# Attention and feed-forward on one core: fewer, wider warming matmuls at the front, and k^T v one block sooner in three units

## The chip, the cores and the metric

The kernel runs on one core of one Trainium2 chip. Time is device microseconds of one execution, from the program's start to its end on that core; less is better. The engines are TensorE (PE in the profile; its weight loads are listed apart as PEld), VectorE (DVE), ScalarE (ACT), GpSimd (POOL) and SyncE (SP). Each runs its own list of instructions in order, and they wait for each other through semaphores. Operands lie in SBUF (128 partitions); TensorE writes to PSUM[...].

## The reference

Linear attention with a norm, followed by a feed-forward layer:

```python
batch, n_heads, seq, head_dim = (8, 8, 576, 64)          # q, k, v in fp32
kv = np.einsum('bhsd,bhse->bhde', k, v)                  # "k^T v", 64x64 per batch and head
out = np.einsum('bhsd,bhde->bhse', q, kv)
rms = np.sqrt(np.mean(out * out, axis=-1, keepdims=True) + 1e-06)
attn_out = (out / rms * g_norm)
x = attn_out.transpose(0, 2, 1, 3).reshape(4608, 512)
h = x @ w_in                                             # 512 x 2048
g = s * np.maximum(h, 0.0) ** 2 + b
return g @ w_out                                         # 2048 x 512
```

All matmuls are in fp32. The weights arrive in pairs of 32-bit words, from which ScalarE (lines 235 and 240) and VectorE (lines 245 and 255) make fp32 values.

## The kernel before, in words

**Units.** The 4608 rows of x are nine units of 512 rows (u = 0 to 8). A unit is its first product (x w_in), the activation, and its second product (g w_out). Both products are done with fewer block products than plain tiling needs, from sums and differences of blocks (`mm1`, `mm1_deep`, `mm2`), except that three quarters of unit 0's first product are plain (`mm1_plain`). The attention rows of unit u + 1 are worked out beside unit u, in two pairs of 256 rows named A and B (`attention_of_two`: `turn`, `product`, `back`, `square`, `row_sum`, `norm`, `turn_x`, `scale`).

**k^T v.** `kv_product(b)` makes the eight 64x64 products of one batch b. A pass over i = 0, 1 takes four heads each; in each, nine steps j over the sequence, two pairs l and two row halves r give 36 matmuls of 64x64, so that four of them sit in different quarters of TensorE's array at once. The result goes through two PSUM banks (`kv_ps`) into `bd_kv[b % 2]`, a block-diagonal matrix, by four copies (ScalarE, line 402; for b = 0 two are on VectorE, line 400). Batch 0 is done at the front; b = 1 in the second product of unit 0; b = 2 in the first product of unit 1; b = 3 at the end of the second product of unit 1; b = 4 to 7 in the first products of units 3 to 6.

**The order of the work** is written out by hand; each engine gets its instructions in the order of the calls. For units 2 and up, `run` in `mm1_deep` lists the calls of the first product, and `at(n)` marks the places where side work is put in; `sides` tells which side work goes where. Around the change it reads, with `x1`, `x6`: four matmuls of 256 columns each and a ScalarE copy; `small(...)`: one level deeper, two matmuls of 128 columns per step:

- `at(4)`: A's `product`, 32 matmuls into two PSUM banks of the pool `ps_t` (line 554)
- `at(5)`: A's `back`, two VectorE transposes out of these banks (line 566), `square` on ScalarE (line 573) and B's `turn` on VectorE (line 542)
- `small(7, 0, 1, 2)`, `small(2, 0, 6, 7)`, `x6(1)`, then `at("kv")`: `kv_product` in units 3, 4 and 6, into the same two banks of `ps_t`, and then `small(7, 0, 6, 7)`

Unit 5 has its k^T v at `at(2)`, and into other banks. k and v for it come through a ring of 14 SBUF slots (`queue_w2`, `pump`, `used`), which SyncE's queue fills in the order of a list: for each unit k and v first, then the weights of the unit. `used` after k^T v frees its slots and lets SyncE issue the next loads.

**The front.** k and v of batch 0 are loaded in two halves (i = 0, 1), each by four transfers shared by the queues of SyncE and ScalarE, then q for the first 512 rows (eight transfers), then the first five weight blocks of 1 MB (SyncE, line 205). Meanwhile `warm` issues matmuls of an identity matrix into a PSUM tile that nobody reads. Before the first half of k^T v there are 18 of 128 columns; between the halves there are four of 128 columns and 42 of 4 columns. After the second half come, for four groups of 128 rows c = 0 to 3: `turn` (transposes of q, line 436), `take` (a copy on VectorE, line 441, or ScalarE, line 443), `product` (lines 92 and 452), `square`, `root`, `norm` (ScalarE lines 463 and 469, VectorE lines 465, 473 and 475), `turn_x` (lines 493 to 509), mixed with the conversion of the first two weight blocks (`hi`, `lo` on ScalarE, `shift`, `plus` on VectorE), and then the first plain products.

The program's list for TensorE has 3,924 matmuls before the change, 24 of them transposes, and 407 separate semaphore waits. In the trace, one matmul of the code is two LDWEIGHTS and two MATMUL records, and a transpose is one of each.

## Time and profile before

| what | us |
|---|---|
| median of three runs | 901.99 (901.68 to 902.92) |
| the profiled execution: its own time | 901.62 |
| the profiled execution: span from first to last instruction | 899.8 |
| TensorE busy in the span | 890.1 (99%) |
| VectorE busy | 697.8 (78%) |
| ScalarE busy | 354.1 (39%) |
| GpSimd busy | 262.7 (29%) |
| mean granted TensorE clock | 0.998 |

A row of the timeline has the start and the length in us, the engine, the line of the kernel, the operation, the tile written and the tiles read, the shape, the number of records merged, and, in brackets, how long the engine had been idle and what ended it. "issue" there means that the engine waited for nothing that the profile shows. Matmuls overlap, so a row's length reaches a little into the next row; the distance of two starts is the time that a row takes. In a table by stretch, each engine has its busy time and number of records, and then come the granted clock, the DMA share and GB/s.

The kernel's chain of work lies on TensorE for 95% of the span; VectorE has 3% of it, and DMA, ScalarE and "issue" 1% each.

### The profile page before, as it was taken

To read this page: it belongs to the slowest core of one execution; us is meant where nothing else is said; L and a number is where in the kernel's file an instruction comes from. 1 tells how busy PE (TensorE), PEld (TensorE's weight loads), DVE (VectorE), ACT (ScalarE), POOL (GpSimd) and SP (SyncE) were. 2 spreads that over 40 slices of the span, in tenths; PEclk is the share of its full clock that TensorE was granted. 3 is DMA by queue.
4 is the path that set the end of the run, shared out by engine and by line. 5 is a ranking of instruction groups with operands and counts; after the bars stand their busy time and mean duration, and the time that the engine had idled before them with its cause. 6 is when DMAs were issued, how large, how long until landed. Compare 5 with 4: busy or idle time off the path is not lost.

```text
span 899.8 us, 20172 instructions
## 1 busy us (share of the span) xinstructions
PE 890.1 (99%) x7824; PEld 826.6 (92%) x7824; DVE 697.8 (78%) x1374; ACT 354.1 (39%) x612; POOL 262.7 (29%) x493
## 2 busy tenths in 40 slices
PE   8999999999999999999999999999999999999998
PEld 7788888888899998999899999999999989999998
DVE  1899778786597977797788878897779787975696
ACT  1887124531266105630455026701761066205610
POOL 2017147213664023800472037403530300021000
PEclk9999999999999999999999999999999999999999
DMA  9797828539973996389656984597639822993286
GB/s 263 256 341 237 238 70 281 179 105 338 300 229 84 303 327 177 91 257 309 204 136 192 305 280 108 136 323 243 192 99 308 299 78 59 295 306 102 60 280 189
DMA packets 124110, 192.98 MB, mean 214 GB/s; under 512 B 25712, under 2 KB 43504, under 8 KB 124016
## 3 DMA queue, kind: packets, MB, share of 16 engines
q1 hardware_dynamic: 104048, 165.84, 58.4%
q0 software_dynamic: 16512, 23.63, 9.3%
q10 hardware_dynamic: 3456, 2.23, 1.0%
q8 instruction: 62, 1.02, 0.5%
q14 instruction: 32, 0.26, 0.1%
HBM read 164.37 MB, written 27.26 MB: 213 GB/s over the span
## 4 chain that ended last, share of the span: by engine, by line
PE 95%; DVE 3%; DMA 1%; ACT 1%; issue 1%; DVEq 0%; ACTq 0%
PE x_ps L92 46%; PE y_ps L92 25%; PE z_ps L92 11%; PE sx_ps L92 6%; PE st_ps L92 2%; PE kv_ps L386 2%; PE y_ps L554 2%; DMA kv_sb<-in_v_dram 1%; PE warm_ps L92 0%; DVE xT L598 0%; DVE xn L587 0%; DVE xs L263 0%; DVE ss L465 0%; PE z_ps L386 0%; DVE xn L475 0%
## 5 line engine op out<-in xcount | busy, mean ns | idle before, releaser
L1694 POOL DMA_DIRECT2D q_sb<-in_q_dram x296 | 167.2, 573 | 85.7 <-ACT r L928 44.1
L1274 POOL DMA_DIRECT2D out_dram<-o x120 | 59.6, 503 | 354.7 <-issue 210.5
L92 PE MATMUL x_ps<-w_sb,sub 128*128 128x128 f32 x1176 | 148.5, 275 | 0.0
L92 PEld LDWEIGHTS x_ps<-w_sb,sub 128*128 128x128 f32 x1176 | 139.8, 192 | 0.0
L653 ACT ACTIVATE a<-a,b_col,s_col 128x512 f32<-128x512 f32 x144 | 117.0, 813 | 27.0 <-DVE a L656 18.6
L853 ACT COPY a<-x_ps 128x512 f32<-128x512 f32 x28 | 16.3, 582 | 243.1 <-PE x_ps L92 243.1
L92 PE MATMUL x_ps<-xs,ws_raw 128*128 128x256 f32 x384 | 91.1, 380 | 0.1
L92 PE MATMUL x_ps<-xT,wa 128*128 128x256 f32 x360 | 84.1, 382 | 0.1
L92 PE MATMUL y_ps<-xs,wb 128*128 128x256 f32 (+1 forms) x360 | 80.0, 365 | 0.0
L92 PEld LDWEIGHTS x_ps<-xs,ws_raw 128*128 128x128 f32 x384 | 69.5, 190 | 8.3 <-ACT r L727 0.5
L92 PEld LDWEIGHTS x_ps<-xT,wa 128*128 128x128 f32 x360 | 66.6, 190 | 10.7 <-issue 1.7
L966 ACT ACTIVATE a<-a 128x512 f32<-128x512 f32 x112 | 69.6, 621 | 5.5 <-DVE a L267 5.5
L92 PEld LDWEIGHTS y_ps<-xs,wb 128*128 128x128 f32 x360 | 62.9, 190 | 9.1 <-issue 2.3
L92 PE MATMUL x_ps<-w_sb,a 128*128 128x128 f32 (+1 forms) x432 | 64.9, 298 | 0.0
L92 PE MATMUL y_ps<-w_sb,a 128*128 128x128 f32 (+1 forms) x416 | 62.4, 295 | 0.0
L92 PEld LDWEIGHTS x_ps<-w_sb,a 128*128 128x128 f32 x432 | 58.4, 192 | 2.9 <-issue 0.4
L92 PEld LDWEIGHTS y_ps<-w_sb,a 128*128 128x128 f32 x416 | 56.0, 192 | 2.1
L260 DVE TENSOR_TENSOR r<-sx_ps,a 128x256 f32<-128x256 f32 x84 | 35.3, 420 | 22.4 <-PE sx_ps L92 22.0
L260 DVE TENSOR_TENSOR r<-x_ps,o 128x256 f32<-128x256 f32 (+1 forms) x84 | 29.7, 354 | 28.4 <-PE x_ps L92 27.7
L92 PE MATMUL y_ps<-w_sb,sub 128*128 128x128 f32 x392 | 49.5, 275 | 0.0
L92 PE MATMUL z_ps<-w_sb,a 128*128 128x128 f32 (+1 forms) x352 | 46.9, 280 | 0.0
L263 DVE TENSOR_TENSOR a<-a,a 128x512 f32<-128x512 f32 x72 | 46.7, 683 | 0.1
(232 smaller groups left out, 1659.0 us busy)
## 6 DMA issues: line engine op xcount, KB each, us to landing
w_sb<-w SPq DMA_DIRECT2D x427, 256.0 KB, 4.9
w_sb<-w SPq DMA_DIRECT2D x14, 512.0 KB, 9.9
w<-sub POOLq DMA_DIRECT2D x28, 256.0 KB, 6.0
out_dram<-o POOLq DMA_DIRECT2D x112, 64.0 KB, 4.4
w_sb<-in_k_dram SPq DMA_DIRECT2D x24, 288.0 KB, 5.2
w_sb<-in_v_dram SPq DMA_DIRECT2D x24, 288.0 KB, 5.3
w_raw<-in_moe_w_in_dram SPq DMA_DIRECT2D x6, 1024.0 KB, 6.8
q_sb<-in_q_dram POOLq DMA_DIRECT2D x160, 32.0 KB, 3.9
```

What stands on the lines that cost most here:

```text
L92: nc.tensor.matmul(o, lhsT=lhsT, rhs=rhs, start=start, stop=stop, skip_group_check=True)
L260: nc.vector.tensor_tensor(out=o, in0=a, in1=b, op=ALU.add)
L263: nc.vector.tensor_tensor(out=o, in0=a, in1=b, op=ALU.subtract)
L386: nc.tensor.matmul(ps[r][(r ^ l) * HB : (r ^ l) * HB + HB, i, :], lhsT=kv[l][0][rows, j, :], rhs=kv[l][1][rows, j, :], start=(j == 0), sto ...
L554: nc.tensor.matmul(ps[l][32 * p : 32 * p + 32, r, lo:hi], lhsT=bd_kv[b % 2][rows, p, at : at + 32], rhs=st["qT"][rows, p, lo:hi], start=Tr ...
L653: nc.scalar.activation(t, t, AF.Identity, scale=s_col, bias=b_col)
L853: nc.scalar.copy(g_tile("a11", s), st["x", s])
L966: nc.scalar.square(ga[name, s], ga[name, s])
L1274: queues[s % 2].dma_start(out=view[b, jj, :, cols], in_=st[name, j][s * w : s * w + w, cols])
L1694: load()
```

## The change

`warm` makes matmuls of 512 columns: the identity matrix is read four times side by side as the moving operand, by a broadcast, and a whole PSUM bank is written. Before the first half of batch 0's k^T v there are four of them, for 18 of 128 columns; between the halves one, for four of 128 and 42 of 4. So TensorE's list has 59 matmuls less. In `run`, the place `at("kv")` goes ahead of `x6(1)`; it holds side work in units 3, 4 and 6 only. The lists of the other engines have the same instructions; on ScalarE the four copies of k^T v in these units change places with the copy of `x6(1)`. All lines after 362 move up by one or two.

```diff
-    def warm(n, tiny=0):
+    def warm(n):
 
         ps = ps_f.tile([P, 2, TB], FP32, name="warm_ps", tag="z", bufs=1)
+        ps = ps.rearrange("p b (m c) -> p (b m) c", c=P)
         for _ in range(n):
-            matmul(ps[:, 0, :P], ident, ident, True, True)
-        for _ in range(tiny):
-            matmul(ps[:4, 0, :4], ident[:, :4], ident[:, :4], True, True)
+            matmul(ps, ident, ident.unsqueeze(1).to_broadcast((P, 4, P)), True, True)
...
         for i in range(2):
             if b == 0:
-                warm(*((18,), (4, 42))[i])
+                warm((4, 1)[i])
...
             small(2, 0, 6, 7)
+            at("kv")
             x6(1)
-            at("kv")
             small(7, 0, 6, 7)
```

## The prediction, as it was put on record

> **What bounds the kernel now.** I read the page's busy times first, then TensorE's timeline from 0 to 35 us, the chain of waits there, the granted clock by stretch, and last the three places that the reordering touches.

> ```profile
> span 899.8 us, 20172 instructions
> PE 890.1 (99%) x7824; PEld 826.6 (92%) x7824; DVE 697.8 (78%) x1374; ACT 354.1 (39%) x612; POOL 262.7 (29%) x493
> ...
> q8 instruction: 62, 1.02, 0.5%
> ```

> TensorE (PE) is busy 890.1 of 899.8 us, so whatever comes off its path is gained, and there are only 9.7 us of gaps. The last line is a queue of its own that brings in TensorE's instructions: 1.02 MB in 62 packets, 16 KB each. TensorE's timeline shows where the gaps lie: nearly all at the front (columns: start us, length us, engine, line, operation, tiles, shapes, count, and in brackets the idle time and what ended it).

> ```profile
> 1.36 6.30 PE L92 MATMUL warm_ps<-ident 128*128 128x128 f32 x36 [1.36 <-POOL ident masks.py:199]
> 7.59 0.33 PE L386 MATMUL kv_ps<-kv_sb 64*64 64x64 f32 x2
> 8.92 1.27 PE L386 MATMUL kv_ps<-kv_sb 64*64 64x64 f32 x70 [1.00 <-DMA kv_sb<-in_v_dram]
> 10.12 3.33 PE L92 MATMUL warm_ps<-ident 128*128 128x128 f32 x92
> 13.38 0.56 PE L386 MATMUL kv_ps<-kv_sb 64*64 64x64 f32 x21
> 15.45 1.45 PE L386 MATMUL kv_ps<-kv_sb 64*64 64x64 f32 x51 [1.51 <-issue]
> 16.83 1.11 PE L436 MATMUL qT_ps<-ident,q_sb 128*128 128x128 f32 x4
> ...
> 23.47 0.63 PE L493 MATMUL xT_ps<-ident,xn 128*128 128x128 f32 x4 [1.54 <-DVE xn L475]
> ```

> Three things are to be seen. The second warming block takes 3.3 us between the halves of the first k^T v. Then the second half stops for 1.51 us after 21 of its 72 matmuls with nothing to wait for ("issue"). And from 16.83 the attention of the first 512 rows begins. The granted clock by stretch (last three columns: clock as a share, DMA share, GB/s) adds that the stop is followed by half speed:

> ```profile
> 9.10:12.40 3.30, 3.30 (x126) 3.11 (x122) 0.00 (x0) 0.00 (x0) 0.95 (x2) 1.00 1.14 307
> 12.50:15.80 3.30, 1.79 (x81) 1.63 (x81) 0.00 (x0) 0.00 (x0) 0.00 (x0) 1.00 1.17 254
> 15.90:19.20 3.30, 3.28 (x47) 2.79 (x37) 1.27 (x3) 0.89 (x3) 0.00 (x0) 0.50 0.97 320
> ```

> The first number group is TensorE: busy 1.79 of 3.30 us in the stretch with the stop, then a stretch at 0.50. Between 23 and 35 us the chain lies on ScalarE and VectorE, which convert the first weights and normalise; from 35 us it is TensorE almost alone.

> [...]

> **Where the block boundaries lie.** In the records one matmul of the code is two weight loads and two matmuls, so four instructions; a transpose is two. Counted from TensorE's first, with its event semaphores, the stop comes after 3 + 72 + 1 + 145 + 184 + 1 + 43 = 449 instructions (start; 18 warming; semaphore; first half; 46 warming; semaphore; 21 matmuls and 22 loads). If 449 is a boundary, the others are 193 + 256n: up to 16,060 that makes 62, the number of packets. A second sign: in unit 4, k^T v starts at 438.59, 86 instructions before such a boundary; the next row starts 2.28 us later for 290 instructions, so the boundary is passed at 439.27, and the packet begins between 439.7 and 439.8. So the fetch begins about 0.5 us after its boundary where DMA is idle. At the front it begins at 13.0 to 13.1, some 3.2 us after its boundary (about 9.9), with DMA full, and TensorE resumes 2.4 us after that. A block is there 2.9 us (0.5 + 2.4) to 5.6 us after the previous boundary; k^T v burns 256 instructions in 2.0 us. It is the only work here that can outrun its fetch: the moment is when a boundary falls in the first 34 of its 290 instructions, so that the next one is inside too.

> **The change part by part.**

> *Warming before the first half*: [...] The first half's last data comes 7.25 us after 1.53, at 8.78, and warming ends at 7.4 now. It costs nothing either way: that wait covers it up to 8.8.

> *Warming between the halves*: 3.26 us become one matmul of 512 columns. The 128-column rows start 111 ns apart at full clock, so four times that, twice: 0.89 us, from 10.12 to 11.0. Then what is late next is the second half's data: the last v piece is issued at 3.14 and the slowest landing of these loads is 9.1 us, so 12.2; the first half started 0.14 us after its data. The second half starts at 12.4 instead of 13.38: 1.0 us gained, not 2.4.

> *The stop*: the front is now 236 instructions shorter (59 matmuls). Boundary 193 lies 23 into the second half, and 449 some 135 after its end, among the small products of the third 128 rows, about 19 us. The fetch starts at 12.5 and needs at most 5.6 us: 18.1. The 1.51 us go. There the cover is only about 1 us, but what follows waits on ScalarE anyway.

> *Together* the second half ends, and the transposes start, at 12.4 + 1.45 = 13.85 instead of 16.83: 2.98 us. The q loads they need have landed (the latest of the first pair by 14.0).

> *Who is late next.* ScalarE's first weight conversion (line 235) starts at 23.12; 2.98 sooner is 20.14. The first weight load is issued by SyncE at 12.82 and lands in 7.2 us: 20.0. Both agree, so even if the attention ran at full clock (two groups of transposes and two of products, about 0.5 us each less), ScalarE could gain no more than 3.1. VectorE's first conversion, at 24.67, follows those two ScalarE steps (1.25 us): 21.4, up to 3.3 sooner. The next loads land by 22.9 to 31.4 and are used at 27.4, 36.2 and later, so they stay hidden. From there ScalarE and VectorE have no gaps over 0.3 us until TensorE takes over at 35: it moves by 3.0 to 3.3; I take 3.1.

> *k^T v one block sooner* (units 3, 4, 6): its 72 matmuls and four ScalarE copies change places with x6(1), four matmuls of 256 columns and one copy. Sum of TensorE's work: unchanged. It now starts at 341.70 in unit 3 instead of 343.52. It waits for the two VectorE transposes out of its PSUM banks, which end at 341.28: 0.4 us of cover, the same in units 4 and 6. Behind a late one stands x6(1). Its loads stand in SyncE's queue ahead of weights that TensorE has used before; freeing the ring's slots starts the next loads 1.8 us sooner, while POOL's queue is not passed. I take 0; bounds 0 and +0.4 us each if the cover is short.

> *Places in the count.* All later code moves by 236, which is 20 against the boundaries, and units 3, 4, 6 by 16 back. The first boundary lay 201, 110, 193, 138, 86, 131, 108 instructions into the seven later k^T v; it will lie 181, 90, 173, 134, 82, 111, 104 in. None is under 34. The tightest, 82: 208 instructions at 7.9 ns, then 48 more at 1.82 us (16 of x6) and about 2.2 us: 5.6 us, about what 86 had without a stop.

> **Sum.** Against its own time, 901.62 us (span 899.8 and 1.8 around it): 901.62 - 3.1 = 898.5. The median of the runs shown is 901.99, 0.4 above: 898.9; I say 898.8.

> **Rivals.**
> - *Full gain, and more* (0.08): no stretch at 0.50 any more, and the loads land sooner too. A gain of 4.3: 897.6. Against it, the 20.0 us landing.
> - *Half clock in the first weight products* (0.14): the warming that filled 10.1 to 13.4 is gone and TensorE now idles from 11.0 to 12.3 and between attention steps[...]. If half speed falls on 23 to 27 us, up to 1.7 us are lost, less 0.6 us of waits there: gain 1.4 to 2.4, 899.6 to 900.5. Against it: 2.30 of 3.30 us busy (5.7 to 9.0) did not lower the clock.
> - *The front is hidden anyway* (0.05): weights or conversions bind at the old time; 901.5. Against it: the conversions run back to back after attention.
> - *Slower: stops inside later k^T v* (0.05). If the boundaries really lie some 80 instructions earlier, four blocks (units 1, 4, 5, 6) have both boundaries inside, 1.5 us each: 4 x 1.5 - 3.1 = +2.9, 904.9. It decides from 34 instructions down, and three blocks are enough for a loss. Against it: before, 86, 108 and 110 would have been caught too, and show no gap.

> **How the numbers follow.** My forecast, 898.2 to 899.4, gets 0.68. The range 897.6 to 900.4 adds the larger gain and most of the half-clock case: about 0.85 with its fringes taken off, 0.8. About 0.2% (1.8 us, so 900.2) is what a measurement of this kernel can tell from no change: faster 0.84 (the first two cases and half to two thirds of the half-clock one), same 0.11, slower 0.05.

> **What would show it.** Right: the second half in one row from 12.4, no idle "issue" in it; transposes by 13.9; the first ScalarE conversion at 20.1; k^T v in units 3, 4, 6 of 2.3 us without idle time, its first VectorE wait unseen. Wrong: a stop near 19 us or in a later k^T v; a stretch at 0.50 over 23 to 27 us; second-half data later than 12.2; an idle stretch before the moved blocks.

## The result, and the profile after

| kernel | median us | runs | ratio to before, 95% interval |
|---|---|---|---|
| before, in the same session | 902.52 (901.38 to 902.92) | 8 | |
| after | 899.06 (898.25 to 900.25) | 8 | 0.9964, 0.9954 to 0.9975 |
| after, a second session (before there: 901.92) | 899.10 (898.49 to 900.89) | 9 | 0.9971, 0.9961 to 0.9981 |

The change gains 3.2 us (2.3 to 4.2, from the ratio of the first session). The profiled execution took 898.25 us, 3.37 below the one of before; its span is 3.3 shorter. The page begins:

```profile
span 896.5 us, 19936 instructions
PE 886.0 (99%) x7706; PEld 819.3 (91%) x7706; DVE 697.4 (78%) x1374; ACT 353.6 (39%) x612; POOL 262.2 (29%) x493
...
q8 instruction: 61, 1.00, 0.5%
```

TensorE has 118 matmul records less, two for each of the 59 matmuls. The packets of its instructions (q8, 62 before) are no measure of the change: the warming alone, with a list of the same length, has 62. TensorE's timeline of the front, after (start us, length us, and in brackets the idle time and what ended it):

```profile
1.36 5.97 PE L92 MATMUL warm_ps<-ident 128*128 128x512 f32 x8 [1.36 <-POOL ident masks.py:199]
...
10.10 1.13 PE L92 MATMUL warm_ps<-ident 128*128 128x512 f32 x2
12.14 1.61 PE L385 MATMUL kv_ps<-kv_sb 64*64 64x64 f32 x72 [0.91 <-DMA kv_sb<-in_v_dram]
13.68 0.66 PE L435 MATMUL qT_ps<-ident,q_sb 128*128 128x128 f32 x4
...
20.04 0.63 PE L492 MATMUL xT_ps<-ident,xn 128*128 128x128 f32 x4 [1.54 <-DVE xn L474]
...
23.21 3.72 PE L92 MATMUL x_ps<-xT,wa 128*128 128x256 f32 x16
27.20 1.97 PE L92 MATMUL y_ps<-xT,wb 128*128 128x256 f32 x8 [0.27 <-DVE inv L472]
```

The second half is one row of 72 records: no "issue" inside it. It now waits 0.91 us for its own v, so the data sets its start. The transposes begin at 13.68 (before: 16.83), and the first plain product at 23.21, 3.42 sooner than before:

```profile
26.63 3.72 PE L92 MATMUL x_ps<-xT,wa 128*128 128x256 f32 x16
```

In a second profile of the same kernel, taken with the experiments, the two begin at 13.97 and 23.56, so the plain product comes 3.07 sooner there. ScalarE's timeline shows the step that I had named as the next late one, before and after:

```profile
23.12 0.67 ACT L235 ACTIVATE w_raw<-w_raw 128x512 f32<-128x512 f32 x1
```

```profile
19.23 0.56 ACT L442 COPY qT<-z_ps 128x512 f32<-128x512 f32 x1
20.32 0.69 ACT L235 ACTIVATE w_raw<-w_raw 128x512 f32<-128x512 f32 x1 [0.52 <-DMA w_raw<-in_moe_w_in_dram]
```

After, ScalarE waits 0.52 us for the first weight block; before, it didn't wait there. VectorE's first conversion follows an attention step of its own there, without idle time:

```profile
20.64 0.69 DVE L474 TENSOR_TENSOR xn<-y_ps,inv 128x512 f32<-128x512 f32 x1
21.25 0.42 DVE L245 TENSOR_SCALAR wa<-w_raw 128x512 uint32<-128x512 uint32 x1
```

The stretches that held the stop and the half speed, after:

```profile
12.50:15.80 3.30, 2.47 (x80) 2.19 (x81) 1.27 (x3) 1.10 (x3) 0.00 (x0) 1.00 1.10 244
15.90:19.20 3.30, 2.61 (x24) 2.37 (x22) 1.48 (x3) 1.56 (x4) 0.00 (x0) 1.00 0.98 333
```

TensorE is busy 2.47 us of the first one (1.79 before), and the second is at full clock (0.50 before). All of TensorE's waits of more than 0.25 us, after (what waited, for what, us in total, times, longest):

```profile
PE kv_ps L385 <- DMA kv_sb<-in_v_dram: 2.3, 2, 1.4
PE xT_ps L492 <- DVE xn L474: 1.5, 1, 1.5
PE warm_ps L92 <- POOL ident masks.py:199: 1.4, 1, 1.4
PE x_ps L92 <- DVE qT L440: 0.8, 1, 0.8
PE y_ps L92 <- DVE wb L255: 0.3, 1, 0.3
PE y_ps L92 <- DVE inv L472: 0.3, 1, 0.3
```

None of them lies after 30 us, and none is "issue". Matched matmul by matmul, TensorE runs 3.43 us sooner than before up to unit 3, and 3.36 from there to the end: everything is gained at the front, and 0.07 goes where k^T v was moved (nothing in the second profile, which runs 3.12 sooner on both sides of it).

### The profile page after: what moved, and what is told of

It is laid out like the page before. It is cut to its first block, busy times and chain, and to the rows that moved or that the text cites. A ratio compares the mean times of both kernels' runs of the same rounds, so it can differ in the third digit from the quotient of the medians.

```text
span 896.5 us, 19936 instructions
## 1 busy us (share of the span) xinstructions
PE 886.0 (99%) x7706; PEld 819.3 (91%) x7706; DVE 697.4 (78%) x1374; ACT 353.6 (39%) x612; POOL 262.2 (29%) x493
## 4 chain that ended last, share of the span: by engine, by line
PE 95%; DVE 3%; DMA 1%; ACT 0%; issue 0%; SPq 0%; DVEq 0%
PE x_ps L92 47%; PE y_ps L92 25%; PE z_ps L92 11%; PE sx_ps L92 6%; PE st_ps L92 2%; PE y_ps L553 2%; PE kv_ps L385 2%; DMA kv_sb<-in_v_dram 1%; DVE xT L597 0%; DVE xn L586 0%; DVE xs L263 0%; DVE xn L474 0%; SPq L107 0%; PE z_ps L385 0%; DVE ss L464 0%
## 5 line engine op out<-in xcount | busy, mean ns | idle before, releaser
L92 PE MATMUL x_ps<-w_sb,sub 128*128 128x128 f32 x1176 | 148.5, 275 | 0.0
L92 PEld LDWEIGHTS x_ps<-w_sb,sub 128*128 128x128 f32 x1176 | 139.8, 192 | 0.0
L92 PE MATMUL x_ps<-xs,ws_raw 128*128 128x256 f32 x384 | 91.4, 381 | 0.1
L92 PE MATMUL x_ps<-xT,wa 128*128 128x256 f32 x360 | 84.1, 382 | 0.1
L92 PE MATMUL y_ps<-xs,wb 128*128 128x256 f32 (+1 forms) x360 | 80.0, 365 | 0.0
L92 PEld LDWEIGHTS x_ps<-xs,ws_raw 128*128 128x128 f32 x384 | 69.5, 190 | 8.5 <-ACT r L726 0.5
L92 PEld LDWEIGHTS x_ps<-xT,wa 128*128 128x128 f32 x360 | 66.6, 190 | 10.7 <-issue 1.7
L92 PEld LDWEIGHTS y_ps<-xs,wb 128*128 128x128 f32 x360 | 62.9, 190 | 9.1 <-issue 2.3
L92 PE MATMUL x_ps<-w_sb,a 128*128 128x128 f32 (+1 forms) x432 | 64.9, 298 | 0.0
L92 PE MATMUL y_ps<-w_sb,a 128*128 128x128 f32 (+1 forms) x416 | 62.4, 295 | 0.0
L92 PEld LDWEIGHTS x_ps<-w_sb,a 128*128 128x128 f32 x432 | 58.4, 192 | 2.9 <-issue 0.4
L92 PEld LDWEIGHTS y_ps<-w_sb,a 128*128 128x128 f32 x416 | 56.0, 192 | 2.1
L92 PE MATMUL y_ps<-w_sb,sub 128*128 128x128 f32 x392 | 49.5, 275 | 0.0
L92 PE MATMUL z_ps<-w_sb,a 128*128 128x128 f32 (+1 forms) x352 | 46.9, 280 | 0.0
```

Source lines behind the costliest of these rows:

```text
L92: nc.tensor.matmul(o, lhsT=lhsT, rhs=rhs, start=start, stop=stop, skip_group_check=True)
```

## The experiments

Four questions were open: which half of the change brings the gain; whether the stop really follows from the place in the count; how the front's gain splits into its parts; and what stands in the way next. Each kernel was timed beside the kernel before, whose medians were 902.11, 902.06 and 901.92 us in the three sessions.

**Each half of the change alone.** The warming alone, with the wide matmuls of the changed `warm`:

```diff
-                warm(*((18,), (4, 42))[i])
+                warm((4, 1)[i])
```

> The five wide warming matmuls alone; k^T v stays behind x6(1). Theory (the gain lies in the front alone, and the order around k^T v is worth nothing): 899.1 us, ratio to the kernel before 0.996, the first half-array row of the second half at 12.1 without an idle stop. In units 3, 4 and 6 the first instruction block boundary then falls 118, 66 and 88 instructions into k^T v; at 66 there are 32 more instructions after k^T v before the next, about 4.2 us after the first against 2.9 us that a fetch took in quiet stretches: no stop there, or one of under 1 us. Rival (the earlier place is a part of the gain): 900 to 902 us. Second rival (the earlier place costs, since k^T v then waits for VectorE): 898.5 to 898.9.

And the moved k^T v alone:

```diff
             small(2, 0, 6, 7)
+            at("kv")
             x6(1)
-            at("kv")
```

> k^T v ahead of x6(1) in units 3, 4 and 6 alone; the front is that of the kernel before. Theory: 902.5 us, ratio 1.000 within 0.001, the stop of 1.5 us in the second half of the first k^T v still there, since its place in the count is the same. Rival (the move is a part of the gain): under 901.5 us. Second rival (it costs 0.1 us in each unit): 902.8.

Measured: 899.28 us for the first (ratio 0.9973, 0.9962 to 0.9983), 901.89 for the second (0.9999, 0.9991 to 1.0007). So the gain is the warming's; the move alone is worth nothing within 0.1%. With the move alone the front keeps its stop, as TensorE's timeline of that kernel shows, and a stretch at half clock behind it:

```profile
10.45 3.33 PE L92 MATMUL warm_ps<-ident 128*128 128x128 f32 x92
13.72 0.56 PE L386 MATMUL kv_ps<-kv_sb 64*64 64x64 f32 x21
15.51 1.76 PE L386 MATMUL kv_ps<-kv_sb 64*64 64x64 f32 x51 [1.23 <-issue]
```

**The place in the count.** Tiny matmuls ahead of the first half (they fit into its wait for data, or nearly) shift every later block boundary by four instructions each, and change nothing else (`warm` gets its argument `tiny` back for it). A boundary is a place 193 + 256n in TensorE's count of instructions, and an instruction block is what lies between two of them. The 62 packets of before for some 16,060 instructions (259 each) agree with the step of 256, and these runs test it:

```diff
-                warm((4, 1)[i])
+                warm(*((4, 20), (1,))[i])      # 20 tiny matmuls: shift 80
+                warm(*((4, 28), (1,))[i])      # or 28: shift 112
+                warm(*((4, 12), (1,))[i])      # or 12: shift 48
```

> The changed kernel with 20 more warming matmuls of 4 columns ahead of the first half, 0.5 us that the wait for its data hides; they shift everything later by 80 instructions. By the count, boundaries of 256 instructions then fall 101, 10, 93, 54, 2, 31 and 24 instructions into the seven later k^T v (batches 1 to 7). Theory (a block that is used up before the next has been fetched stops TensorE): stops inside k^T v of batches 2, 5, 6 and 7 and in no other, 0.9 to 2 us each, 4 to 8 us in all: 903 to 907 us. Rival (the stop at the front came from the small matmuls or from data, and places in the count mean nothing): 899.1 us, no idle stop in any later k^T v.

> The same with 28 small matmuls, a shift of 112 instructions. The boundaries fall 69, 234, 61, 22, 226, 255 and 248 instructions into the k^T v of batches 1 to 7. Theory: a stop in batch 4 (22), one in batch 6 (its boundaries lie 1 instruction before the block and 255 into it), a short one or none in batch 7 (8 before, 248 in), and none in batches 2 and 5, which stop with 20 small matmuls: 2 to 5 us in all, 901 to 904 us. Rival (the places mean nothing): 899.1 us. Second rival (small matmuls ahead of the first half cost by themselves): the same time as with 20 of them, or more, with no stop inside batches 4 and 6.

> The changed kernel with 12 matmuls of 4 columns ahead of the first half: every later boundary moves by 48 instructions against k^T v. First boundary in the later blocks (batches 1 to 7): 133, 42, 125, 86, 34, 63 and 56 instructions into each. It looks for the edge of the zone that stops a block. Theory (a stop only if this number is 34 or less, so that the next boundary is inside the block's 290 records, and only in a block that TensorE reaches without a lead): at most batch 5, with its second boundary on the block's last instruction, stops for 0 to 1.2 us; time 899.0 to 900.3. Rival (what counts is whether 256 instructions go by within 2.9 us of a boundary, so blocks with 42, 56 and 63 stop as well, at the work right behind them): three or four stops of 0.5 to 1.3 us, 901 to 903.

Measured:

| shift | median us | ratio, interval | "issue" in all, us | k^T v blocks with a stop inside or right behind: batch (place of a boundary before or inside it, place of the stop) |
|---|---|---|---|---|
| 0 (after) | 899.10 | 0.9971, 0.9961 to 0.9981 | 0 | none |
| 48 | 899.61 | 0.9975, 0.9965 to 0.9984 | 1.0 | 5 (34; at 290, right behind it) |
| 80 | 902.00 | 1.0003, 0.9995 to 1.0011 | 2.9 | 5 (2; 260), 6 (31; 288), 7 (24; 282) |
| 112 | 903.35 | 1.0012, 1.0005 to 1.0018 | 4.9 | 3 (61; 317, behind it), 4 (22; 280), 5 (30 before; 228), 6 (1 before; 256), 7 (8 before; 250) |

The waits for "issue" of the kernel with shift 80:

```profile
PE kv_ps L387 <- issue: 2.1, 2, 1.1
...
PE y_ps L387 <- issue: 0.8, 1, 0.8
```

the one behind batch 3 with shift 112 (at 238.93 us):

```profile
PE x_ps L92 <- issue: 0.6, 1, 0.6
```

and a stop in TensorE's timeline of the kernel with shift 112, and in that of the kernel with shift 48:

```profile
339.80 2.31 PE L387 MATMUL kv_ps<-w_sb 64*64 64x64 f32 x138
343.16 0.34 PE L387 MATMUL kv_ps<-w_sb 64*64 64x64 f32 x6 [1.05 <-issue]
```

```profile
434.03 2.34 PE L387 MATMUL kv_ps<-w_sb 64*64 64x64 f32 x144
437.40 1.78 PE L92 MATMUL x_ps<-xs,ws_raw 128*128 128x256 f32 x7 [1.03 <-issue]
```

The nine stops of the table come at most two instructions from where the count of 193 + 256n puts them, so in these runs the boundary is shown as their cause. Shift 80 has three stops where four were expected, of 2.9 us in all instead of 4 to 8. Among the executions with a mean granted clock of 1.000, the medians are 899.04 (after), 901.86 (shift 80) and 903.70 (shift 112): 2.8 and 4.7 us more, for 2.9 and 4.9 of "issue". So 20 matmuls that cost next to nothing themselves eat the whole gain of the change.

What ends a stop can be read from the instruction packets, one for each boundary (62 in before). I take the one that begins near a boundary for the one needed after the next; no record says what a packet holds, but the times fit. In the stop of before it runs from 13.07 to 14.16 us, after the boundary at 9.74, and TensorE goes on at 15.45, at the next boundary. In all 12 stops of these traces TensorE goes on 1.3 to 1.5 us after the end of this packet, and at none of some 780 other boundaries did it get there less than 1.28 us after it. So in these traces a stop comes where TensorE reaches the next boundary before its packet has been there for 1.3 us, and the place in the block is only half of it; when the packet comes is the other half.

In the five blocks with the boundary inside, the packet begins 0.1 to 0.8 us after the boundary is executed, and TensorE goes on 2.9 to 3.3 us after it: 435.21 to 438.47 in one, 339.97 to 343.16 in another. Three things that the rule "in the first 34" didn't foresee belong here. With shift 80, batch 2 has its boundary at instruction 10 and doesn't stop: its packet begins 0.3 us before the boundary is executed (152.65 and 152.94). Why it comes sooner there was not shown. With shift 112 three blocks stop whose boundary lies up to 30 instructions ahead of them, and one stop comes behind batch 3, whose boundary is at 61: these packets begin 0.8 to 2.5 us after their boundary, and the one at batch 3 takes 2.7 us, where most take 1.0. The rival of shift 48, that places 42, 56 and 63 stop as well, falls in that run, where these packets come in time; the place 61 of shift 112 shows that such a place can stop. Why a packet comes early or late is open: in the trace of before they begin from 4.2 us ahead of the execution of their boundary to 6.1 us behind it.

**The parts of the front's gain.** The kernel before with the tiny matmuls moved ahead of the first half, so that the count up to the second half stays as it was:

```diff
-                warm(*((18,), (4, 42))[i])
+                warm(*((18, 42), (4,))[i])
```

> The kernel before, with the 42 matmuls of 4 columns moved from between the halves to ahead of the first half; four of 128 columns stay between. The count of instructions ahead of the second half is unchanged, so boundary 449 still lies 43 instructions into it, and 193 now lies before the first half's products, passed at about 7 to 8 us instead of 9.9. My theory (the front's gain has two parts: 1.2 us from the shorter wait between the halves, 1.5 us from the stop that goes): the second half starts at about 12.2 (its data); the fetch is triggered earlier, so the stop is shorter than 1.5 us, 0 to 1.0, in the same place (instruction 43). Time: 899.0 to 900.5, i.e. 1.6 to 3.1 below before. Rival 1 (only the count of instructions matters; the stop stays as it is, 1.5 us, wherever the second half starts): gain 1.2, 900.9. Rival 2 (the stop was no fetch but followed from the 42 tiny matmuls right ahead of the second half): no stop and the whole gain, 899.1, with no idle time at instruction 43.

And the changed kernel with the old time between the halves, but not the old count:

```diff
-                warm((4, 1)[i])
+                warm((4, 4)[i])
```

> The changed kernel with four matmuls of 512 columns between the halves instead of one: 3.6 us of warming there, 0.3 more than in the kernel before, and the count of instructions only 12 higher than after, so no boundary is near the second half's middle (places of the later blocks 169, 78, 161, 122, 70, 99, 92). It keeps the old time between the halves and takes the stop away. My theory: second half from about 13.7, in one row, without idle time and without a stretch at half clock; it ends at about 15.2, 1.5 later than after; of that some 0.5 us is taken up by the weight landing at 20.3, so 900.1 to 900.6 (+1.0 to +1.5 against after; 1.5 to 2.0 below before). Rival 1 (the time between the halves was the whole of it and the stop cost nothing on the path): as before, 902. Rival 2 (the stop was the whole of it and the weight landing hides the rest): as after, 899.1.

TensorE's timeline, tiny matmuls first:

```profile
10.55 1.28 PE L386 MATMUL kv_ps<-kv_sb 64*64 64x64 f32 x72
11.75 1.16 PE L92 MATMUL warm_ps<-ident 128*128 128x128 f32 x8
12.84 0.56 PE L386 MATMUL kv_ps<-kv_sb 64*64 64x64 f32 x21
15.56 1.03 PE L386 MATMUL kv_ps<-kv_sb 64*64 64x64 f32 x51 [2.15 <-issue]
```

and with the wide middle:

```profile
9.91 3.70 PE L92 MATMUL warm_ps<-ident 128*128 128x512 f32 x8
13.54 1.28 PE L385 MATMUL kv_ps<-kv_sb 64*64 64x64 f32 x72
14.75 0.66 PE L435 MATMUL qT_ps<-ident,q_sb 128*128 128x128 f32 x4
```

The first one went otherwise than expected, by a slip of mine: the 42 matmuls take 2.9 us, not the 1.1 us of room, so the boundary was passed no earlier (9.85 us; before: 9.74). What it shows instead is cleaner. The second half starts 0.54 us sooner than before, and the stop grows from 1.51 to 2.15 us: TensorE goes on at 15.56 instead of 15.45, in both kernels 5.7 us after the boundary and 1.3 us after the packet's end. So in these two kernels the end of the stop doesn't follow from the work ahead of it, and a shorter wait there is lost in a longer stop; the two parts of the gain are not independent. Its median is 900.84 all the same (0.9986, 0.9980 to 0.9993), 1.3 us below before, near the 900.9 of the first rival, whose stop of unchanged length didn't come. The profiled execution has no stretch at half clock here, and its first plain product comes 0.64 us sooner.

The wide middle gave 899.77 (0.9978, 0.9968 to 0.9987), 2.0 us below before with the second half at 13.54, later than before's 13.38. So the stop and what follows from it are some 2 us. The shorter middle brings the rest: in the traces the transposes come at 14.75 and 13.68, and the first plain product at 24.30 and 23.21, 1.1 us (0.7 against the second profile of after); in the medians 0.7.

**The one matmul that is left, or two.**

```diff
-            if b == 0:
-                warm((4, 1)[i])
+            if b == 0 and i == 0:
+                warm(4)
```

> The changed kernel without the one matmul of 512 columns between the halves; four instructions less ahead of the second half (places of k^T v 177, 86, 169, 130, 78, 107, 100 into the block). My theory (the second half starts when its data has landed, about 12.1 us; the middle warming is covered by that wait): same time as after, within 0.3 us, 898.9 to 899.4, second half from 12.1 in one row. Rival 1 (that matmul keeps the granted clock up): a stretch at half clock somewhere in 12.5 to 20 us, up to 1 us slower, 900. Rival 2 (the middle warming is on the path): 0.8 us sooner, 898.3. Place 78 (unit 4) is the tightest: a stop there of up to 0.5 us would be seen as idle time inside that k^T v.

```diff
-                warm((4, 1)[i])
+                warm((4, 2)[i])
```

> The changed kernel with two matmuls of 512 columns between the halves instead of one. They end at about 11.9 us, still before the second half's data (12.1 to 12.9), and keep TensorE busier before it; places of the later blocks 177, 86, 169, 130, 78, 107, 100. Theory (the data sets the start of the second half, and idle time ahead of it risks a stretch at half clock, as without any matmul there): the same as after in its undisturbed executions, and safer: 898.6 to 899.2, no stretch at half clock. Rival (the second matmul delays the second half where the data comes early, and one was enough for the clock): 899.1 to 899.6.

(The places in the first of these expectations have a wrong sign; they are 185, 94, 177, 138, 86, 115 and 108, and no block stops.) Without it: 900.27 us (0.9978, 0.9969 to 0.9986), 1.2 slower than after. TensorE waits for data until 12.78, and then the clock falls, as the stretches of that kernel show:

```profile
9.10:12.40 3.30, 1.27 (x70) 1.15 (x70) 0.00 (x0) 0.00 (x0) 1.14 (x2) 1.00 1.13 300
12.50:15.80 3.30, 3.02 (x80) 2.92 (x80) 0.99 (x3) 0.52 (x2) 0.00 (x0) 0.76 1.16 237
15.90:19.20 3.30, 3.25 (x22) 3.01 (x21) 0.68 (x2) 1.42 (x3) 0.00 (x0) 0.73 0.97 320
```

The half speed lasts from 14.2 to 17.7 us, and it takes 7.13 us instead of 6.36 from the transposes to the first xT. All of its 11 executions had a mean granted clock of 0.998 or less; of the 17 of after, two. So the theory that this matmul is wholly covered falls, and its first rival holds: the matmul is off the path by its duration, and on it by what it does to the clock. The change itself was run again beside the kernel with two:

> The changed kernel unchanged, beside the two others on one chip. 899.1, within 0.4.

Two gave 899.13 us (0.9973, 0.9962 to 0.9984), the change itself 899.10: one is enough, and no version was found that beats the change.

**The next bound.** The first weight load goes ahead of the q of the last two row groups:

```diff
+    send_w()
     load_q(2, two)
-    for _ in slots_of_raw:
+    for _ in slots_of_raw[1:]:
```

> The changed kernel with the first 1 MB weight load put ahead of q of the third and fourth 128 rows in the queue of SyncE. It tests my step that the landing of the first weight block (20.0 to 20.3 us) is what stands behind the front's gain. My theory: it lands 1 to 2 us sooner (two q transfers of 0.25 MB each at about 320 GB/s are 1.6 us); ScalarE's first conversion is then bound by its own attention steps at about 19.8, 0.5 us sooner, and the later q blocks land up to 3 us later (about 19 us), so that the third and fourth 128 rows of attention wait: gain of at most 0.5 us, 898.6, or a loss of up to 2, 901. Rival (the landing binds nothing; the conversions follow the attention): no gain at all, and only the loss from late q, 899.1 to 901.

903.43 us (1.0012, 1.0004 to 1.0020): worse than either case. The load was issued at 10.63 instead of 12.90 and landed at 19.99 instead of 20.29; where it was issued at 12.8 to 13.8, it landed between 19.86 and 21.42, so it came no sooner than in some of those. q came so late that its transposes waited:

```profile
PE qT_ps L435 <- DMA q_sb<-in_q_dram: 3.8, 1, 3.8
```

ScalarE's conversion stands behind the attention of these rows in its own list and started at 24.15. So this run doesn't tell whether the landing binds; the traces of the others do, below.

## Why the prediction held, step by step

1. *Warming before the first half costs nothing*: right. The first half's long row starts at 8.7 to 9.4 in the kernels with the new warming and at 8.92 before, always behind its data.
2. *Between the halves, 1.0 us, and then the data*: right in kind. The second half started at 12.14 instead of the 12.4 of the sum, and at 12.05 to 12.81 in the other profiles with one wide matmul in the middle: its data's landing moves that much from one execution to the next. What the step missed is that little of this would have come through without the end of the stop: with the tiny matmuls first, a second half that starts 0.54 us sooner ends only 0.31 sooner.
3. *The stop goes, 1.51 us*: right, with its cause. Boundary 449 is now executed at 21.3; the packet for what follows came at 14.58 to 15.54. The sum had put the boundary at about 19, with only about 1 us of cover; it is over 4.
4. *Together 2.98 us at the transposes*: 3.15, because the data came a little earlier. Some 0.4 us of it is the clock's: the last 51 matmuls of the second half take 1.38 us before (15.45 to 16.83, at half speed from 15.86), and 0.96 in the kernel with the tiny matmuls first. The sum took them at full speed without naming it.
5. *Who is late next*: the landing was right (20.29 for 20.0), and ScalarE's first conversion gained 2.80, at 20.32 for the 20.14 of the sum. Wrong was to let it cap TensorE. VectorE's first conversion starts at 21.25 (before: 24.67), 3.42 sooner and so more than the "up to 3.3" of the sum: it follows the first ScalarE step alone and not both (the second ends at 21.59), and that takes up ScalarE's wait. From the first xT to the second x_ps row of 16 records TensorE needs 11.52 us in after, and as much in the kernel with the wide middle, where ScalarE doesn't wait (it starts at 20.79, after a landing at 20.07); with shift 48 ScalarE waits 0.72 us, and TensorE needs 11.53. Where the load landed at 21.42 (warming alone) and ScalarE waited 1.23, it did bind: 12.03 us. So the landing binds only a few tenths of a us further on, and not at a gain of 3.1.
6. *k^T v one block sooner, 0*: 0.07 us in unit 3 in one profile, none in the other, nothing that the times show. It starts 0.54 us after the start of the row before it, where a row of this kind takes 0.45; no wait for VectorE is seen. The 0.4 us of cover held.
7. *Places in the count, none under 34, no stop*: right for this change. The rule itself was too narrow: stops came with boundaries from 30 instructions ahead of the block to its 34th, and one behind a block with its boundary at 61, while batch 2 didn't stop with boundaries in that zone (10 in with shift 80, 22 ahead with shift 112). The step that failed in it is the time of the fetch: "0.5 us after its boundary" was read in one block, and the packets of before begin from 4.2 us ahead of their boundary to 6.1 us behind it. Of the cases named against the slower rival, the places 86, 108 and 110 were rightly read.
8. *Rivals*: "the front is hidden" and "stops inside later k^T v" didn't come. "Half clock in the first weight products" didn't come in after, but one matmul less brings half speed, at 14.2 to 17.7 us and not at 23 to 27 (900.27, where the rival said 899.6 to 900.5). "No stretch at 0.50 any more", from the rival with the larger gain, did come, and the sum had no term for it.

The clock's part can be read from the mean granted clock of each execution. The profile of before has one stretch at half speed, 3.41 us from 15.86; that loses 1.7 of 900 us, and its mean is 0.998. So I put 0.002 of the mean down to each such stretch, which is an estimate. Of 107 executions of before in three sessions, 54 had 0.998 (median 901.82 us), 36 had 0.996 (902.83) and 14 had 0.999 or 1.000 (901.12). Of 17 of after, 11 had 1.000 (899.04), and none was below 0.998. By this estimate most executions of before had one stretch, a third had two, and each goes with 0.7 to 1.0 us more; the change takes nearly all of them away. Between executions without one the change gains 2.1 us (901.12 and 899.04), so about a third of its 3.2 us goes with the clock. That is an estimate too: the executions are sorted here and not changed, and what else differs between them is not known. Where the second stretch lies is open, since no profile of before caught it. It also explains a part of why the kernel with the tiny matmuls first gains 1.3 us with its stop intact: 11 of its 21 executions had 0.998 (901.07) and the others 0.999 or 1.000, none 0.996. At the same 0.998 it is still 0.75 us faster than before, and what brings that is open.

The sum said 898.5 for the profiled execution and 898.8 for the median; measured were 898.25 and 899.06. That the median fits so well is in part luck, since the front gained 3.4 us in one profile and 3.1 in the other, and the stretches at half speed had no term. Executions of one kernel differ by 2 us for reasons outside the change, among them the landing of the second half's v, and the last stores, which took 2.3 us longer in the profile of the warming alone than in those of before and after.

## What to carry to other kernels

Before trusting an edit that changes the number of instructions, count where the instruction blocks' boundaries fall in the code that uses up instructions fastest (here k^T v, 256 in 2.0 us; a shift of 80 instructions cost 2.9 us); a stop that the profile calls "issue" in the middle of a run of small matmuls is the sign. In the 12 stops here it ended 1.3 to 1.5 us after the packet that began near the boundary before, and work in between that let TensorE come 0.54 us sooner only lengthened the stop, from 1.51 to 2.15 us. And a warming matmul that ends long before its data can still count: the one here ends at about 11.2 us, 0.9 ahead of its data, and without it the clock fell to half for 3.41 us and the kernel took 1.2 us more. Price it by what the clock does without it, not by its duration.
